# Loading x in four transposing transfers per stage, with a new stored order of the operations, in a fused long-convolution and memory-attention kernel

## The chip, the cores and the metric

The kernel runs on one core of a Trainium2 chip. The core has five engines with instruction streams of their own: TensorE (PE), VectorE (DVE), ScalarE (ACT), GpSimd (POOL) and SyncE (SP). DMAs are issued by SP, ACT and POOL here. The metric is the device time of one execution in microseconds. Before the change its median over 11 runs is 326.55 us (325.63 to 328.15).

## The reference

Two independent computations on sequences of 2048 tokens and 640 channels, laid side by side in the output:

```python
# A: a gated long convolution
k_shift = sum over t of k_pad[:, t:t+S, :] * shift_k[:, ks-1-t]      # ks = 4
kv = k_shift * v
y  = irfft(rfft(kv padded) * rfft(ssm_k padded))[:S] + kv * ssm_D
a  = q * y
# B: attention with a compressive memory, 32 heads of 20, N = 4 stages of L = 512 tokens
for s in range(4):
    a_dot = softmax(qs ks^T * scale + causal mask) vs
    a_mem = phi(qs) M / (phi(qs) z + 1e-6)
    o     = g * a_mem + (1 - g) * a_dot
    M, z  = M + phi(ks)^T vs, z + sum phi(ks)
b = o @ wo
return concatenate([a, b], axis=-1)
```

`shift_k` multiplies taps of the previous tokens, `phi` is x+1 for positive x and exp(x) otherwise, and `g` is a sigmoid of `beta`.

## The kernel before

**Part A** goes over five blocks of 128 channels (`dp`). Each block has its own loads (`load_sk`, `load_kv`, `load_q`), a shift by matmuls on `kr` (`kshift`), forward DFTs of kv ("X") and of the filter ("K") as matmuls with `Wf` (`fwd`), butterflies and a pointwise product on DVE (`bfly`, `pointwise`, `ybfly`), and inverse DFTs with `Wi` (`inverse`) whose results are multiplied by q and stored by POOL.

**Part B** goes over eight units `u`: stage `s = u // 2` of 512 tokens, and half of the heads `u % 2`. `b_proj_chunks` (line 532) makes the operations up to the attention: `load` (line 539, once per stage, in the first half) brings x of the stage into the tile `xT`, transposed, channels on the partitions; `proj(tci)` (line 556) projects 128 tokens to K, Q and V, three groups of five matmuls with `wqkv`, which ACT copies out, and sends K and Q through a DMA transpose into `KQT` (line 567) from one of two buffers `KQ`; `bound` (line 575) makes a bound of the scores by one group of matmuls, copies it as `bT`, and POOL writes it as rows into `KQT` in four small DMAs (lines 592 on); `mem` (line 596) updates the memory. `b_attn_chunks` makes the scores in the PSUM region `st`, their exponentials `ET` on ACT, the product with V, and, after the second half of a stage, four DMA transposes of the result `o_s` into `oT` (`outt`, line 681) and the output projection (`outproj`).

`xT` is one tile with one buffer, [128, 5, 512]. In stage 0 x is loaded as it stands and transposed by PE. In stages 1 to 3 a single DMA transpose on SP's queue fills the whole tile (line 542); it may start when the last projection of the stage before has read the tile, and every projection of its stage waits for it:

```python
if s > 0:
    nc.sync.dma_start_transpose(out=xT[:], in_=self.x[L * s:L * s + L, :])
```

**The order.** No engine instruction is issued where these functions are written. A recorder collects every operation with what it must come after, found from the bytes that it reads and writes; matmuls on one PSUM bank that follow each other are one operation. Then `Recorder.emit` (line 197) issues them in the sequence of `ORDER` (line 703), a stored list of operation numbers that was found offline by a search. So each engine's stream, and SP's and POOL's queues, stand in that sequence, and since every call is made in line 216, all rows of the profile show L216; tiles tell them apart. An engine works its stream in order: an instruction that waits holds up what is behind it. PSUM has one region `st` of four banks and four single banks `w`; `take` and `per_bank` hand them out as the sequence goes.

Of the kernel before, what the change touches and what calls it, by code (L numbers as in the profile page):

```python
# [21 lines left out]
S = 2048; D = 640; C = 512; P = 1024  # L22
# [253 lines left out]
class K3:  # L276
# [255 lines left out]
    def b_proj_chunks(self, u):  # L532
        nc = self.nc
        V = nc.vector
        s, half = u // 2, u % 2
# [3 lines left out]
        def load():  # L539
            xT = self.ring("xT", [128, 5, L])  # L540
            if s > 0:
                nc.sync.dma_start_transpose(out=xT[:], in_=self.x[L * s:L * s + L, :])
            else:
                xn = self.ring("o_s", [128, 4, H, DH])[:].rearrange("p t h d -> p t (h d)")
                nc.scalar.dma_start(out=xn, in_=self.x[0:L, :].rearrange("(t p) c -> p t c", p=128))
                for cc in range(5):
                    px = self.bank("w")
                    for tci in range(4):
                        nc.tensor.matmul(px[:, 128 * tci:128 * tci + 128], lhsT=xn[:, tci, 128 * cc:128 * cc + 128], rhs=self.ident[:], start=True, stop=True)
                    if cc % 2:  # L550
                        nc.scalar.copy(out=xT[:, cc, :], in_=px)
                    else:
                        V.tensor_copy(out=xT[:, cc, :], in_=px)
            self.xT = self.xTs[s] = xT
# [41 lines left out]
        def mem():  # L596
# [10 lines left out]
            V.tensor_tensor(out=dst[:, :, :, 0:DH + 1], in0=src[:, :, :, 0:DH + 1], in1=mt[:, :, :, 0:DH + 1], op=ALU.add)  # L607

        ch = [(load, 0.1)] if half == 0 else []
        ch += [(proj(t), 3.0) for t in range(4)] + [(bound, 4.0)]  # L610
        if s < NS - 1:
# [89 lines left out]
BANKS = {"st": (1, 2048), "w": (4, 512)}  # L701
SUMMED = ("X",)
ORDER = (
    'c-jTQ17H{c3<SVWKAG)x=-k=1jn1~&*|u%lwr$(CZQmtUA`W6BEW#lIA|n!j;!vbUM1)2dI1GYN2#?g7Qj=*Cjf)tFid33H(`Zr+(&U;`b7^+Xp?NhWN^4q8uZa+dbeci4Xmpg-teQ>p'
    'YbxZ^0-8~aY9=kG(NIQ<p_t~@!dg(vYiVTGQplqfw1^hcl3GGbX+^E1Ns$bdH5QViuGZ6FO@rc^6&aBe>5&P!kO66t4cU<yxseVzkOg@VfJr)8M`#I@#7M2CiID^;P+zNPRn3ch$d3j('
    'L91&K6h#e<hbcN$M`?VNLm8CC3>~dwbb(IO@fwVYI#U<wSe>r3v;b!7GF_#sb&jsk<ysiyv;xXwp4QenT1%s#rmobvx>#Fl8=bFzwK}SzA{uICEYTWRs_Qf+)@mgb#ColQYS^i}v=AC;'
    'V{M{MQ6F{DR2!hV*2WY}!bD8Q8eOE#&`d+L9@=YTG(ijPq0LbTJ+&cPpqn;AO?20=tc3~qr{HdFsjYN_Zqkj~R@>=VjKdi0#&`&)VJfC$Cc<;G&OjGcM&K6hs^Qo{J8EkLp(XZcE6hS0'
    '%*A|k(#|>$p&5!{xB&gMzxL9Fh|bw?4$$7Z2yGFSa}b4nG#cBXuSRA}Zp1*1!9g0x1dPQ14%SUb$VB{sxJ=4#NPwUCjvcxa+jP5b)%|)vS7RksVKLTV3HItfU5>R_hZR_ggL+6)u_+Jh'
    'MLnWJv>Df9s9w@#IH?;D!Y=59&e(<23}Q-l#Zf(`X&8_32}#RgI$XQql%`{PCT4qH)rce;GYPM0BqpPA8#W_3w_*#rqbE|Z2YRCyn((sj!AE?>7lfcAGBPtWF#|v0H~!!k{^B1xpgjWR'
    'GY;c4VzVu;XdIr_>v{xdbT7`J9rxje=3*A^$3f)g0UXyu$jWRKq4dE`?T75Vr6xyl94B!?RZid(jv)_2%UN~F%X1n=ZfiG&l2$y6b7;-;+8-CR4ZARr+|lq7St7_?jUqi5Q3mmzCPYit'  # L710
    'kxuN+`x;3eXipBtL(RcQ+KZie0XuLWL-1Jp;)!<UCG_J(<m3<*<zNnFZ{}k$4&XrcWqvki3*JNl7Gz--VNB`30qD=+9Ej~0!I4ZN_2sGd;UElSalX`8Qi89vBVXt}mSja%;z*3)D2~E3'
    'R$wWP=5&tbIF4s&2J^MXmNyzlYOp5nvkWJ2A|LP}AMvf$mZ_Y?$sCF)EXQGZ$=58;=lV?RNnLr$8Jx)*7>?(>jyHV8XRO7_{K_h<&2Nk<b@-VtScp|wjb-_fA6S=P_@1zNj3)J1pYtj9'
    'iMMbYzjz0~`G*a77Y*4|mhvx`F|7Qf+e*IWDu$Ege8&}h%;*wBYRNTR#bwlx!BSJMU<49NL-|Rw2GU5HNMli(#qSKZCk$srZ8mAetfI}~T&`wuD`7vlhI@GraV3m}w@?-!VJ)=9lSYg$'
    '5iFvu<vQNS1MFiY%OvG3v+QRDOCxQhl^kGX+s(AHhfmO2T1Z=IDKV@%V_GbWZDnmeA0nY7m1L4mGDv#KC<_=Q3z<^N*g<aKAui%#K1De@%p-h;jZ7|^m`YMeYH23XEUHDZ=vG}uW2o$x'
    '%{(d1C5vR0A(CCP$s^>HC9Gz@^s9c*ANpH=>O0-SZ~9(8>Q=Us_Ogx1t+XAGLvm26SXB#=4wAxpN=e(!VRBe<NH0ksN4bO5Z6|lJl*O?c7T3B<Evsqut+vIt1lGu2qlq=P239~C+GFIG'
    'mexa>+A-F%W75Ko%5k3L5qX0U3$S=r$C_DhX>N5bsr8YB_F0ozpuNBs&1mhclAYjwJ1!?AktMcP_7ZKZt8|u*lF2^lTRg{ieIc(9WR<O(bdh&RX`SR0(_33>ZyoGCQdtJ;XsPWqJ6UGC'
    '$OD$eE-{zolY-LP(pXw6B>kkX9JJha+z#1Z87{e`vvsvR(#>+qKIvk4WsmHZla|L0+X*{nBP6e7wQQEevRe)-ET`<M<+HPv-_FTs86$nIpPjQaa$btcSt%m@Wq{<g>vrC**$wM&7i_HD'
    'wgNW5#z}9xXnpL86|^HZQI6UOn<OLco(;5gR$K~MVJjv@th5ZW!FE9|$`Csx!)&;Xl*w|Qr{#{_wfpwK9@<bVB^Nl#M#*R!W8-CtOtc9y$;Mi2kLhuIvc>W#HdV&icq<{(<dL1WGxpe~'
    '+D%L7(`}mFvN;y$bFI9@_ZgPJ2T4hJDbr=9%#sQ+LuT46n`dWOMlRWWi|4N;i7&8QGF#?ISvkvvcG(u$ZFy?X?V0`2C-wp5<Q!kvVtZ*-B)LzpMY6<}+AFIlDg3o1^|YSM-`EXF=WlJX'
    '43t!!+HcBdOXFWGqc5{cvQU=DQmHD-WVYRryK<9X?H0e;J9}@J<ez2n5BAY+^9ol;CeP}beYs@wRg&E=%LBP0@T+_%^m}rR=HKnUT$Ss*CO_?m-Qjf+SN~->Jf}zU`SMEUNo83eH+YxT'  # L720
    'WUl1(TplcWJhw;o6}HNj+e-T&U*xGgk>B>mR?1^pEsx}@{E(j#&b!+;Suf!|f`6AD_R0R*23aR-#XXdV_AtIidRkcTWzXcfe3Vb}OCtJb$>+Z%zrT?v9@XE;TPf@BWs{Wi0$$Lgd366H'
    'J0!>p`Bo|HDZQkZ@{Mwt(7*Cec8cm|5smBVJ&|Yd08i|ty@(g}GG5g~YZ%=oVYQft)AC-yi+c$VuQ5E>D|!Ttq!BfWR`YsZ-#1ug-)L2QldZMQR^3-yO|Rh%e2uNMhF;6J+AayDrc~E0'
    'wnetfdTZphy^crLN*+V&dSl;aO?<oUu$|V_ciA4>YrCzPH}@7EU88DCkE5+TrY6+Z9!sNXT#c>!EI`|Oh_~^M-rn1JXYb^J+QGYcSC6OhwTE}}-rn7NdIC+PeZ7zO@_ydm{{zzes$>'
)


# [73 lines left out]
```

## Time and profile before

| | |
|---|---|
| median of 11 runs | 326.55 us (325.63 to 328.15) |
| the profiled execution | 327.24 us, of it span 325.1 us |
| mean granted TensorE clock | 0.963 |
| DMA | 42.58 MB in 89891 packets, 131 GB/s over the span |
| SP's queue (q1) | 78512 packets, 25.91 MB |
| POOL's queue (q0) | 5488 packets, 12.44 MB |

The span runs from the first to the last instruction of the profiled execution. The page gives each engine's busy time in it, the chain of work that ended last followed back from the end, groups of instructions by tile, and DMA issues with their time to landing. `w<-wqkv,xT` is a projection matmul into a bank `w`; `st<-KQT` is a score matmul; `xT<-in_B_x_dram` is the load of x. A row of a wait names who waited, for whom, the total, the number and the longest. A DMA in SP's timeline shows the time that its issue took on the queue's engine, not the transfer; the chain and the DMA rows show the time until it landed.

### The profile page before, as it was taken

What the parts mean: (1) busy time and instruction counts of PE and PEld (TensorE: products, weight loads), DVE (VectorE), ACT (ScalarE), POOL (GpSimd) and SP (SyncE); (2) the same over time, 40 slices, a digit from 0 to 9 for tenths busy, and PEclk for the clock granted to TensorE, in tenths of its full rate; (3) what the DMA queues carried; (4) which work ended last, traced back from release to release, by engine and by line L of the source; (5) the groups of instructions that cost most, each with busy time, mean ns of one, the idle gap of its engine ahead of it and who ended that gap; (6) DMA issues with size and microseconds to landing.
All of it is one profiled execution on the core that took longest, in us unless ns stands there. A gap on an engine that the chain in (4) does not pass through costs nothing.

```text
span 325.1 us, 11830 instructions
## 1 busy us (share of the span) xinstructions
PE 283.4 (87%) x5182; PEld 202.2 (62%) x5182; DVE 248.3 (76%) x382; ACT 259.1 (80%) x347; POOL 82.5 (25%) x138
## 2 busy tenths in 40 slices
PE   2849979999998997997999996499899999887984
PEld 2536557677676775664787774167667676664662
DVE  1135761898997877999989879139999999899951
ACT  2255489989998996999979996179997999886822
POOL 8000200610550001306430045400041036103333
PEclk9997999999999998999999999599999999996999
DMA  8799967577973979357536999834019456102255
GB/s 213 178 229 192 238 154 140 141 153 191 211 191 117 148 128 159 87 87 159 146 70 122 131 172 186 171 62 73 2 34 135 105 127 115 40 18 67 78 111 155
DMA packets 89891, 42.58 MB, mean 131 GB/s; under 512 B 78928, under 2 KB 85776, under 8 KB 89712
## 3 DMA queue, kind: packets, MB, share of 16 engines
q1 hardware_dynamic: 78512, 25.91, 44.7%
q0 software_dynamic: 5488, 12.44, 15.0%
q10 hardware_dynamic: 5840, 3.49, 4.6%
q8 instruction: 40, 0.66, 0.9%
q14 instruction: 11, 0.09, 0.1%
HBM read 14.16 MB, written 5.24 MB: 60 GB/s over the span
## 4 chain that ended last, share of the span: by engine, by line
PE 34%; issue 18%; DMA 17%; ACT 16%; DVE 9%; ACTq 2%; POOL 2%; SPq 1%; DVEq 0%; POOLq 0%
PE w L216 30%; ACT ET L216 7%; PE st L216 5%; DMA KQT<-KQ 4%; DMA xT<-in_B_x_dram 4%; DMA kr<-kr 3%; DMA KQT<-bT 2%; DVE S L216 2%; DMA out_dram<-outa 2%; ACTq L216 2%; ACT KQ L216 2%; ACT PqT L216 2%; ACT F L216 2%; POOL out_dram L216 1%; DVE Kh L216 1%
## 5 line engine op out<-in xcount | busy, mean ns | idle before, releaser
L216 ACT ACTIVATE ET<-st 128x2048 bf16<-128x2048 f32 (+1 forms) x96 | 155.2, 1617 | 11.1 <-PE st L216 10.1
L216 PE MATMUL w<-wqkv,xT 128*128 128x320 bf16 x480 | 79.6, 312 | 9.5 <-DMA xT<-in_B_x_dram 7.5
L216 PEld LDWEIGHTS <-xT 128*128 128x128 bf16 x480 | 45.5, 101 | 33.6 <-DMA xT<-in_B_x_dram 7.8
L216 ACT CAST F<-w 128x512 bf16<-128x512 f32 x80 | 46.0, 620 | 8.1 <-PE w L216 7.6
L216 PEld LDWEIGHTS <-ET 128*128 128x128 bf16 x1280 | 40.0, 96 | 8.5 <-issue 6.6
L216 PEld LDWEIGHTS <-Wf 128*128 128x128 bf16 x400 | 36.8, 99 | 11.4 <-issue 4.5
L216 PE MATMUL w<-Va,ET 128*128 128x21 bf16 x1280 | 42.8, 173 | 1.2 <-ACT Va L216 0.4
L216 ACT CAST KQ<-w 128x320 bf16<-128x320 f32 x64 | 26.4, 439 | 19.7 <-PE w L216 15.9
L216 DVE TENSOR_TENSOR S<-S 128x2048 bf16<-128x2048 bf16 (+1 forms) x40 | 37.4, 944 | 0.2
L216 PE MATMUL w<-vt,Wf 128*128 128x256 bf16 x240 | 35.6, 275 | 0.6 <-ACT KQ L216 0.5
L216 PEld LDWEIGHTS <-later 32*128 32x128 bf16 x1536 | 19.3, 92 | 25.8 <-issue 23.8
L216 PE MATMUL st<-KQT 21*128 21x512 bf16 (+3 forms) x512 | 34.8, 300 | 0.0
L216 POOL DMA_DIRECT2D KQT<-bT x32 | 16.5, 519 | 70.4 <-ACT bT L216 38.9
L216 PE MATMUL st<-later 32*128 32x32 bf16 (+1 forms) x1536 | 26.9, 180 | 7.4 <-ACT ET L216 6.7
L216 POOL DMA_DIRECT2D out_dram<-outa x20 | 15.9, 798 | 61.9 <-DVE outa L216 44.5
L216 PE MATMUL w<-wo,oT 128*128 128x320 bf16 x160 | 26.5, 312 | 2.9 <-DVE outa L216 1.7
L216 DVE RECIPROCAL rr<-w 128x32 f32<-128x32 f32 (+1 forms) x32 | 10.5, 327 | 19.9 <-PE w L216 19.4
L216 POOL DMA_DIRECT2D vt<-in_A_v_dram x16 | 12.4, 777 | 48.3 <-PE w L216 47.0
L216 PE MATMUL w<-kT,Wf 128*128 128x256 bf16 x160 | 23.7, 281 | 0.7 <-DVE o L216 0.5
L216 DVE TENSOR_TENSOR S<-Xh,Kh 128x4096 bf16<-128x4096 bf16 x10 | 22.7, 2283 | 0.1
L216 ACT CAST outb<-w 128x320 bf16<-128x320 f32 x32 | 13.3, 440 | 10.9 <-PE w L216 10.8
L216 PEld LDWEIGHTS <-oT 128*128 128x128 bf16 x160 | 15.3, 100 | 10.1 <-issue 4.2
(75 smaller groups left out, 430.7 us busy)
## 6 DMA issues: line engine op xcount, KB each, us to landing
qd<-in_A_q_dram POOLq DMA_DIRECT2D x20, 128.0 KB, 4.1
out_dram<-outa POOLq DMA_DIRECT2D x20, 128.0 KB, 3.1
out_dram<-outb POOLq DMA_DIRECT2D x16, 160.0 KB, 2.8
vt<-in_A_v_dram POOLq DMA_DIRECT2D x16, 128.0 KB, 3.7
kT<-in_A_ssm_k_dram POOLq DMA_DIRECT2D x4, 512.0 KB, 6.4
kr<-kr SPq DMA_DIRECT2D x10, 198.0 KB, 4.1
kr<-kr SPq DMA_DIRECT2D x5, 264.0 KB, 5.0
Wf<-c_wf ACTq DMA_DIRECT2D x4, 256.0 KB, 6.9
```

The costliest lines, as they stand in the source:

```text
L216: f(*fargs, **fkw)
```

## The change

The load of x in stages 1 to 3 becomes four DMA transposes of 128 tokens each, still on SP's queue, each into its own quarter of the tile. The recorder sees nine more operations, and each quarter depends only on the projections of its own 128 tokens. The stored sequence is replaced by another one, found by a search in which the assumed landing times of transfers were lengthened per kind of transfer. Nothing else differs.

```diff
         def load():
             xT = self.ring("xT", [128, 5, L])
             if s > 0:
-                nc.sync.dma_start_transpose(out=xT[:], in_=self.x[L * s:L * s + L, :])
+                for t in range(4):
+                    nc.sync.dma_start_transpose(out=xT[:, :, 128 * t:128 * t + 128], in_=self.x[L * s + 128 * t:L * s + 128 * t + 128, :])
...
 ORDER = (
-    'c-jTQ17H{c3<SVWKAG)x=-k=1jn1~&*|u%lwr$(CZQmtUA`W6BEW#lIA|n!j;!vbUM1)2dI1GYN2#?g7Qj=*Cjf)tFid33H(`Zr+(&U;`b7^+Xp?NhWN^4q8uZa+dbeci4Xmpg-teQ>p'
...
+    'c-jTQ17HvU5Czb?fB$kVyOwP%+qP{ko6ELs+qP}nw%vP)VG>(nNhAp;k)^mqkN^=0BN4?#C6rLYOBx9+VI>WcAqi3;IpRoaM3HC`T~Z(^(jp~tA{T;?1L=?+g^@_IA{&xQcH~2T<VI;^'
...
 )
```

Decoded, the new sequence has the same operations as the old one, with the nine new transfers, at moved places. On every engine neighbours are exchanged over short distances, and many stretches are unchanged. Places that the prediction speaks of, in the new build:

- Start: on ACT's stream the activation table load stands before the first copy of `xT` and the load of V's weights behind it, and three of the four `Wf` loads follow the copies; before, two of them and all of `wqkv`'s first half stood ahead of the table load. On SP the K weights of the second half (`loadw1`) stand third instead of ninth. On PE the first projections are P0.2 Q, P0.2 K, P0.1 K, P0.3 Q, P0.2 V, P0.4 K, P0.1 Q (unit.token block and what is projected) where they were P0.2 Q, P0.2 K, P0.4 K, P0.1 K, P0.1 Q; a projection of unit 1 comes before the memory update of unit 0.
- Stage 2: SP's queue has quarter 1 of x, an `oT` transpose, a `kr` transpose, quarter 0, quarter 2, an `oT` transpose, a `kr` copy, quarter 3.
- Stage 3: quarter 0, two `KQT` transposes, a `kr` copy, quarter 2, an `oT` transpose, a `kr` copy, three `oT` transposes, quarter 1, quarter 3. Before, the load stood behind all four `oT` transposes and three of the five `kr` copies.
- POOL, at the same place: the first of the four rows from `bT`, two stores of `outa`, the other three rows, then loads. Before, loads of q and v stood between the rows.
- DVE: several additions of the pointwise product and of `ybfly` of block 2 stand ahead of the first score matmuls of unit 5.

More of the change, by code (lines that the diff above doesn't have):

```diff
@@ L703 @@
 ORDER = (
-    'c-jTQ17H{c3<SVWKAG)x=-k=1jn1~&*|u%lwr$(CZQmtUA`W6BEW#lIA|n!j;!vbUM1)2dI1GYN2#?g7Qj=*Cjf)tFid33H(`Zr+(&U;`b7^+Xp?NhWN^4q8uZa+dbeci4Xmpg-teQ>p'
-    'YbxZ^0-8~aY9=kG(NIQ<p_t~@!dg(vYiVTGQplqfw1^hcl3GGbX+^E1Ns$bdH5QViuGZ6FO@rc^6&aBe>5&P!kO66t4cU<yxseVzkOg@VfJr)8M`#I@#7M2CiID^;P+zNPRn3ch$d3j('
-    'L91&K6h#e<hbcN$M`?VNLm8CC3>~dwbb(IO@fwVYI#U<wSe>r3v;b!7GF_#sb&jsk<ysiyv;xXwp4QenT1%s#rmobvx>#Fl8=bFzwK}SzA{uICEYTWRs_Qf+)@mgb#ColQYS^i}v=AC;'
-    'V{M{MQ6F{DR2!hV*2WY}!bD8Q8eOE#&`d+L9@=YTG(ijPq0LbTJ+&cPpqn;AO?20=tc3~qr{HdFsjYN_Zqkj~R@>=VjKdi0#&`&)VJfC$Cc<;G&OjGcM&K6hs^Qo{J8EkLp(XZcE6hS0'
@@ L708 @@
[L708 to L723, printed above, removed]
+    'c-jTQ17HvU5Czb?fB$kVyOwP%+qP{ko6ELs+qP}nw%vP)VG>(nNhAp;k)^mqkN^=0BN4?#C6rLYOBx9+VI>WcAqi3;IpRoaM3HC`T~Z(^(jp~tA{T;?1L=?+g^@_IA{&xQcH~2T<VI;^'
@@ new lines @@
+    'Kt_~BUZj#TD2J$$2XUo@WI<^uh(aiWikO7*$b{5V03}cXB~c2M5GaWynN&s<6h$#)Mm?mJ43bgmqd2M}i8MfUR6`1hDGiZaa!M}ACg~)-1W68=jO>zI^2i8`L?+21C8d<alfqI&reG>+'
+    'pe9BkzLb%&Qch-IG_uNgWR?k-h*_A4RTzV1SdA4ZCd;uBV^LJ5VF4Cm9Ohsi=3+YLW4AzNqoU-Me3D-ZNI|KMx~PL%Sd0o%UfQ57D#;R5mKst;s!2_$D%E8vV#qoak|t=1W>Qa@OMPjC'
+    '#%Lmqq=hs?V`(bQu@)`RK-#0FbU+<xiN9Ebe-K-QDKbeW%4Df44W&CGSS{&+h*n!B$XFRK<D|Xplrb_*rpr`On<+CS811kDZDl=Lp*7mbMr=YWX)P&bGj;;D3%jug?WBurL05ExSy=0c'
+    'NJi_4UT_PrPUw#i#I)Y%gD^G#vm~5#mCgun(X9*SOEl|?7}gI9WUkDXIg-fcNmLt%L5OV&C6*<y!H8o?EU_iE9oUBL*ot6TB=IeU{g7|6OZLc5`7Zl$0E=a%td%9QPWECSTG~cgEeFxc'
@@ new lines @@
+    'R>>MUgynJ=>1>5;k|8*Pix`UavQ#c%nViH1=`7u(yQH^-md4Ur4+*pkHVmn3I5OH%9K#mrC7WfN^prl*Tl&f=bh1nq%9`6%WVV#n*&<sDyM`zh+LBpvyNs{$M}EsM`6qv+gLIOP@<l#M'
+    '77Ns@mff=1UimDaB(WZrxOQ5uAf6qO)97H=u}{w6xZFTT+bXH;CPZ%`L{7*V$!qy+zZ{i=a!5|fF*%MPQ_W$a6>54wPT-WBMSgQFVCQffIW3ok(ROxLsG&62&dGVSxBhYg&GZiXSa=Q4'
+    '2znQhHKGo+dq^k=q^)(cdfLnGBa#l5-u3`}?ICj8BlNTLl1RJT5a}m9?1DVT6YP+lc2O=#9vf~YtiKJj)>hC)SV<dfL#&Xsu>n@t23iptWTUN^6}K+d)kawi9UvjrK<nyLl(N?-Z83F>'
+    '4V3LN(`MO7tD`UQ$eyFVKD5X73=Q>(HPWi~2Gwl5m9dwoY-Mevyh1D;YZGjujk8Hs&dS>$sbaCUj@7lv_SBx+Gn-;BtfEb~X*R>A+G`snv+btLu^aN%D%nSSZ^Pu1eXx2~-F{mQt8Z^?'
@@ new lines @@
+    'xLlW__RebBA8TMgEs8d@TK3I;*>|g8x8#Q{w6E64Lb0($)kPMX$`wYgw6N+7r)%t`eYUl>%3j$QTW!(wul=*=Domo`*i;*96Ro9JrG}1>nmSnD;<D7%(K1x#+B_@E>MTdFi8Zxmc3X^h'
+    '<gUcgdlFY8GoD6b6b3LVYcLGw+d5lsr5Tnfb%7nQGHkB#b%SlRXpF!Xno18^Ypu%68l71*JU3ZwYoiY&BCD~jrqvkSXX$jm#bvO@V@qwN={2cl&}6#U4%uN_Vn=MV9kuwpFArs@Ewkm8'
+    'fXD2(oz%*FD#>+=rO+#KO=9wy#AY1s*I3+Y8MP8KX=+WQAMgWT@eA8*yM03ye#B4I;cpDlteQ=O^pRxOy3C<DwS#ul9oA0U>rQ)z_ejfh+-1GAJQL_{+he`;pdQwWJf?@VHizi}J*r3a'
+    'C=)V}4cSBMvk@yW36rt`Te3A1v8T3T8zyEwCe+7LK=;}cIbp9QzrK;??4y0PDckWg8nYRbu?fE*HCwPf(=a*PGMFzUh+SBdC-gW^+HpN)XY8~c;|Zo<O1_k??8MIO#%|h0J82Gn!gmbS'
@@ new lines @@
+    '=kh|+vlib;XU)K~)?Ksly>w?rp0n)isy&#AJ(-hN>?CvXsuf^9?ZC_|s9Bhbg|wfBXn#G$f;`Q=x?A&VF5Rbjv=3j&Tj|T*?8V%=M=$Ua3-Jsu^E@xIFmp2xN9#Eqqj{N+=QS$_Xkjg)'
+    'MYXsN()=u@MR<)xIb28RJr3p&Ugu3d;0@m5L*D05KH*p$sl_;q<8+h`<RIQ<ah~NwJ;!mJq~rOVXY`boU`Z{>QaYR?cv?$qN1oM@9L4cEh8OgbP1TD!mX~dsPT*vn#EG1u(>XzBa558l'
+    'LQm{78R)Z^(qFI?U-BuZ@D-o2gihsj9nF_IOK0dzea$z#!mFIkN1V$!e9T2m<%^lz=P`ws*ZG{S6?6fYu#Dd3d0WcYn#`B+mfqn7Th0}n#(`Q^=jbARr62g7Z~2bp^n?7tMZ2vZxssn)'
+    'RabE}7jm&y)6e|E44%;|X*y5uUzy#r`ZuQaAkX4|n9ct(moL;MT3PStUA>}L^&h`e{EpqVAI$4Zb(yZvHT=n6T(0>%zvuQ<n#T+H1HGX)HH=@kdwNO3`hAVy_w0s6^vinR)UT;I{Gndg'
@@ L724 @@
+    'a30=o+AS;S^g<rXA6Rvrs}*&g&esK6)Qfo$FYK{>EjMr-*Yk@$(UrPdpQ?K(|EfRqr$+OB{HE*mgGTol{$1DTW9`onuGL2x$pid1L;C=3(8wOeqxy4wrt9>he$rnW(?4r*|E(oFj=$5m'
+    '{zj|$d#&zob)#Oh+g3&6d3;acJ9MZ1(UM-ux9TP>?U_7>m+?xT*>iej7yQ$|s@SYRSZvcU2#qA3+S7Paui|CBoLBYwUc+m8EidmCJRB-|Z4ZwKh=ho!;|;upxAcvy>zi25cW@gUdSl<t'
+    'M!uP?d?#D`7B=zS+@%J`79~PqyKdz!?qM5m>rK6xM@DlGK(HTRJ8$nDyrb{sAs*&F9%NKRL3BhzC-3a>5CgH%#bY8q;$S~xp@(<#gy`-)y{q^3z8;9UIKp1u&--`+Btm~5=pjDD2lyZ#'
+    '=0kn35BCxN9|FR!J^'
 )
```

## The prediction

> **What bounds the kernel now.** The page comes first. No engine is saturated over the whole span.
>
> ```profile
> PE 283.4 (87%) x5182; PEld 202.2 (62%) x5182; DVE 248.3 (76%) x382; ACT 259.1 (80%) x347; POOL 82.5 (25%) x138
> ```
>
> The matmul records overlap, so I priced TensorE (PE) by start-to-start spacing in the trace instead: 0.69 us for five projection matmuls, 0.88 for eight DFT matmuls, 0.45 for a score block, 0.79 for the large value block, and so on over all 427 PE operations. That is 267 us of work. PE's first matmul starts at 5.2 and its last ends at 320.3, so about 48 us are lost, mostly in pieces under 1 us where PE waits for ScalarE (ACT) or VectorE (DVE). The waits of PE show the one large piece.
>
> ```profile
> PE w L216 <- DMA xT<-in_B_x_dram: 7.5, 1, 7.5
> PE st L216 <- ACT ET L216: 6.7, 18, 0.7
> ```
>
> Columns: total us, times, longest. Eighteen waits for ACT's exponentials are short; the wait for x is one of 7.5 us. The chain that ended last, read between 186 and 222 us, says which transfer it is.
>
> ```profile
> 195.02 0.29 PE w L216 x2
> 195.31 12.65 DMA xT<-in_B_x_dram
> 207.96 0.04 issue
> 208.00 1.51 PE w L216 x5
> ```
>
> This is the third transposed load, that of the last stage (s=3). It takes 12.65 us from issue to landing; the other two landed in 5.6 and 6.3. SyncE's own timeline shows why:
>
> ```profile
> 191.62 3.60 SPq L216 DMA_TRANSPOSE oT<-o_s  x1
> 195.31 6.98 SPq L216 DMA_TRANSPOSE xT<-in_B_x_dram  x1
> ```
>
> An issue that costs 1.2 to 1.3 us elsewhere costs 3.60 here, and that of x 6.98: the queue is backed up by the copies of kr, four oT transposes, and GpSimd's loads. Everybody pays, as the busy times by stretch show (length, PE, PEld, DVE, ACT, POOL, granted clock, DMA share, GB/s):
>
> ```profile
> 200.00:203.50 3.50, 0.55 (x5) 0.18 (x2) 3.43 (x6) 1.16 (x2) 3.40 (x6) 0.82 1.36 207
> 203.50:208.00 4.50, 0.00 (x0) 0.00 (x0) 0.97 (x3) 0.00 (x0) 2.54 (x5) 0.50 1.10 220
> 208.00:212.00 4.00, 4.00 (x33) 1.89 (x34) 0.00 (x0) 2.14 (x2) 0.68 (x1) 0.50 0.30 75
> ```
>
> PE, ACT and DVE all stop, and PE comes back at a granted clock of 0.50. From 216 on DVE is the fullest engine (19.76, 19.58, 18.78 and 19.72 us of each 20 from 220 to 300), so what is lost here isn't caught up. Before that, ACT is (18.4 to 19.9 of 20 in most stretches).
>
> **The split itself.** One 640 KB transpose per stage becomes four of 160 KB, so nine more DMAs in three stages. The trace has this very shape from another source.
>
> ```profile
> oT<-o_s SPq DMA_TRANSPOSE x16, 3.6
> xT<-in_B_x_dram SPq DMA_TRANSPOSE x3, 6.3
> ```
>
> An oT transpose is 128 x 5 x 128, as a chunk of x will be; it lands in 2.6 to 9.4 us, median 3.6. Its issue is 1.25 us, so four are 5.0 against 2.7 to 3.0 for an undisturbed load of x: 2 us more of SyncE per stage, 6 in all. They run one behind the other without adding up: the last four oT are issued in 310.62 to 315.79, and the matmuls that read them run from 313.84 on without a wait for a DMA.
>
> The Trainium skill speaks against this part: "DMA: Bandwidth & Descriptors", Rules for kernel authors, says to coalesce many small transfers into one large one, and its Anatomy section fits about 2.0 us fixed plus bytes at 436 GB/s on the GpSimd path. By that, if nothing overlapped, nine more transfers would be an estimated 18 us. The oT rows say that they overlap; no row of this trace shows chunks read from HBM.
>
> What the split buys is that a chunk waits only for the projection that reads the same 128 tokens. I took, on PE, the work listed between the last reader of the old chunk and the first reader of the new one (sum of spacings). For stage 3 before: 8.4 us for the whole load, which needed 12.65. After: 20.8, 10.1, 20.9 and 15.5 for chunks 0 to 3. Chunk 1 is the tight one: SyncE's listing has an oT, a kr copy and three more oT between the chunk issued before it and itself, 6.8 us of issues of which 4.3 pass before it may start, so 2.5 of the 10.1 are gone; 7.6 are left against 3.6 (median) to 9.4 (worst oT, in just this crowded stretch). Left over: 0 to 1.8 for the landing, more if the backed-up issues recur. I take 1.0.
>
> Stage 2: before 7.7 for the whole load, which landed in 6.3 and wasn't waited for. After, chunk 0 is tight: 9.5 less three issues (3.75) is 5.8, against 3.6 to 9.4: 0 to 3.6, taken as 0, as DMA is lighter there (109 to 123 GB/s against 207 to 220). Stage 1 has 13.9 or more for every chunk: 0.
>
> **What goes:** the stall, 7.45; and the slow clock behind it. After 208.00 three blocks of five projection matmuls and one score block start 1.45, 1.30, 1.21 and 0.66 us before what follows, where the warm spacing is 0.69, 0.69, 0.69 and 0.43: 2.1 us. Both on the path, as all engines stand.
>
> **What is late next.** The score matmuls of the following unit need rows that GpSimd writes into KQT from bT:
>
> ```profile
> 200.10 1.05 POOL L216 DMA_DIRECT2D KQT<-bT  x2 [2.10 <-ACT bT L216]
> 203.93 0.53 POOL L216 DMA_DIRECT2D KQT<-bT  x1
> ```
>
> The last is issued at 203.93 and such rows land in 6.2 us in this stretch, so about 210.1: 11.6 after the matmul they derive from ended (198.5). PE has 9.7 us of work listed in between, in both builds. So without the stall PE would be about 1.9 early. After, two stores and no loads stand between the four rows, 0.8 us shorter. I charge 1.0 (0 to 1.9).
>
> **The reordering elsewhere.** Prices and PE's total are unchanged, and outside the places named here the listing is that of before with neighbours exchanged, so I cost it by bounds. Start:
>
> ```profile
> 15.80 6.66 DMA KQT<-KQ
> 24.97 1.32 PE w L216 x16
> ```
>
> The projection of the third token block can't be copied out until this transpose frees its buffer; PE then waits until 24.97. After, two more blocks precede the Q projection that this transpose needs (1.3 us each at the slow clock there, 0.7 at the full), and a 400 KB weight load (4.0 to 4.9 us to land elsewhere on this queue) is put ahead of it. Against that, one of the two Wf loads issued just there (15.30 and 16.66) moves ahead, the activation table load moves before the copies of xT (up to 0.6 gained), and one projection block fills the hole (0.7 gained). Between -1.3 and +5; I take +1.5, nearer to the small terms.
>
> DVE: before, it stops with work at hand. Time, us, instruction, idle before it:
>
> ```profile
> 204.16 0.32 DVE L216 TENSOR_TENSOR o_s<-o 128x320 bf16<-128x320 bf16 x1
> 216.25 0.36 DVE L216 RECIPROCAL rr<-w 128x32 f32<-128x32 f32 x1 [11.78 <-PE w L216]
> 217.39 1.21 DVE L216 TENSOR_TENSOR S<-S,pr 128x2048 bf16<-128x2048 bf16 x1
> ```
>
> S<-S,pr had its inputs by 202.9 but stands behind rr. After, the stage from the bound matmul of unit 5 to its first scores lists 18.4 us of DVE work instead of 10.3, and what follows lists 94.2 instead of 102.1; ACT's 96.4 there is the next limit. This stretch takes 106.6 us now. Worth 0 to 5.7 (102.1 less 96.4); I take 2.0, nearer to none, because PE's small waits stay.
>
> **Sum**, against the profiled execution's 327.24 us (span 325.1, 2.14 around it): -7.45 - 2.1 + 1.0 (chunk 1) + 1.0 (bT rows) + 1.5 (start) - 2.0 (DVE) = -8.05, so 319.2. The median of the runs before is 326.55, 0.7 under the profiled one; I keep the larger base and say 319. All terms at their good end: 327.24 - 7.45 - 2.1 - 1.3 - 5.7 = 310.7. All at their bad end: 327.24 - 9.55 + 1.8 + 3.6 + 1.9 + 5 = 330.0.
>
> **Rivals.**
> 1. *The queue, not the size, is the delay.* For: the x packets stood behind oT's, and chunks 1 and 3 are again last on SyncE, at about the same time as the load before. If chunk 1's issue is backed up like the 3.60 and 6.98 above, it lands some 5 us late, the clock drops again, and only 3 to 4 us are gained: about 323.5. Against: chunks 0 and 2 and most kr copies go earlier. 0.14.
> 2. *Given back elsewhere.* The stall goes, but the start takes its 5 us, stage 2 its 3.6 and the DVE gains nothing: 327.24 - 9.55 + 1.0 + 1.0 + 5 + 3.6 = 328.3, or within 0.3% if one of them is smaller. For: the start's transpose is on the chain. Against: 0.7 of PE work fills the hole. 0.09 that it ends within 0.3%.
> 3. *Slower: a stall per chunk.* Each chunk is a DMA of its own with its own place in a queue that also holds oT, KQT and kr. If each read of x from HBM lands in some 12.65 us, as the load of stage 3 did, chunk 0 of stage 2 misses by 12.65 - 5.8 = 6.9 and chunk 1 of stage 3 by 12.65 - 7.6 = 5.1, each with 2.1 of slow clock: 327.24 - 9.55 + 6.9 + 5.1 + 4.2 + 1 = 334.9. It decides from a landing above about 11.5 us in both stages. Against: x landed in 5.6 and 6.3 elsewhere, whole. 0.15.
>
> Forecast 0.62, the rivals 0.14, 0.09, 0.15. Faster by over 0.3% (1 us, about what a measurement of this kernel can tell from no change) is the forecast and the first rival: 0.76; within 0.3% 0.09; slower 0.15. The range runs from 313, between the sum and its good end, to 327, leaving out the slower case and a few per cent below.
>
> **What would show it.** Right: no single PE wait for xT above 2 us; the clock at 1.00 from 195 to 215; DVE's largest idle time there under 4 us; a wait of st for the bT rows of at most 2. Wrong: a wait for xT at stage 2; PE's block now at 24.97 starting after 28; chunk issues of 3 us or more on SyncE; or waits of PE for ACT well above 6.7 in total, which would mean that the exchanged neighbours cost more than I can see here.

## The result, and the profile after

| | before | after |
|---|---|---|
| median of the executions beside each other | 326.83 us (47: 323.43 to 335.12) | 324.30 us (12: 318.20 to 329.54) |
| the profiled execution | 327.24 us, span 325.1 | 326.76 us, span 325.0 |
| mean granted TensorE clock in it | 0.963 | 0.970 |

The ratio after/before is 0.981, 95% interval [0.977, 0.986]; ratios with intervals here compare only executions within 1.5% of the fastest of their kernel, which leaves out 8 of the changed kernel's 12, while medians and ranges are over all. By medians it is 324.30 / 326.83 = 0.992. So the change gains 0.8 to 1.9%, less than the 2.3% that were forecast (319 against 326.55), and its time scatters over 11 us; a further set of six executions gained nothing by medians (after_again, below). The profiled execution lies in the upper part of that range: it shows what goes wrong in such a one, not what a 318 us execution looks like.

The waits of the changed kernel (total us, times, longest):

```profile
PE st L216 <- ACT ET L216: 8.4, 21, 0.8
PE w L216 <- DMA xT<-in_B_x_dram: 7.1, 1, 7.1
DVE o_s L216 <- DMA oT<-o_s: 3.9, 1, 3.9
```

The wait for x is still there, 7.1 us in one piece where it was 7.5. The chain that ended last and SP's timeline say which transfer it is now:

```profile
189.68 5.77 DMA out_dram<-outa
195.45 14.56 DMA xT<-in_B_x_dram
210.06 2.85 PE w L216 x10
```

```profile
189.86 5.49 SPq L216 DMA_TRANSPOSE oT<-o_s  x3
195.45 5.53 SPq L216 DMA_TRANSPOSE xT<-in_B_x_dram  x2
```

Quarters 0 and 2 were issued at 178.08 and 186.63 and are there: the first projection of stage 3 starts at 200.91 instead of 208.00. But the second needs quarter 1, issued at 195.45, and this quarter of the load takes 14.56 us, longer than the whole load before (12.65). The second starts at 210.06; before, it started at 210.11. The stall has moved by one token block. The stretches by busy time (length, PE, PEld, DVE, ACT, POOL, granted clock, DMA share, GB/s) are those shown of before:

```profile
200.00:203.50 3.50, 2.78 (x39) 1.50 (x35) 2.17 (x4) 3.08 (x4) 2.45 (x4) 1.00 1.20 122
203.50:208.00 4.50, 0.00 (x0) 0.00 (x0) 1.86 (x3) 0.99 (x2) 0.53 (x1) 0.83 1.16 144
208.00:212.00 4.00, 1.94 (x8) 1.14 (x9) 1.50 (x3) 0.00 (x0) 2.57 (x4) 0.50 1.34 192
```

PE does nothing from 203.5 to 208, and from there the clock is at 0.50 again. Look at the last two columns. The DMA share adds up the times of all packets that start in a stretch, over the 16 engines, so it can exceed 1. In the first two stretches it is about as high as before (1.20 and 1.16, before 1.36 and 1.10), yet 122 and 144 GB/s move where 207 and 220 did. GpSimd's timeline shows what else was put on them:

```profile
190.46 0.65 POOL L216 DMA_DIRECT2D kT<-in_A_ssm_k_dram  x1
193.46 1.50 POOL L216 DMA_DIRECT2D vt<-in_A_v_dram  x2 [2.36 <-PE w L216]
197.44 1.49 POOL L216 DMA_DIRECT2D qd<-in_A_q_dram  x2 [2.48 <-DVE outa L216]
198.91 0.75 POOL L216 DMA_DIRECT2D vt<-in_A_v_dram  x1
199.65 0.75 POOL L216 DMA_DIRECT2D qd<-in_A_q_dram  x1
200.39 0.53 POOL L216 DMA_DIRECT2D KQT<-bT  x1
...
205.90 0.53 POOL L216 DMA_DIRECT2D KQT<-bT  x1 [2.58 <-DMA vt<-in_A_v_dram]
208.43 1.02 POOL L216 DMA_DIRECT2D KQT<-bT  x2 [2.00 <-DMA qd<-in_A_q_dram]
```

After kT (512 KB), six loads of 128 KB are issued between 193.5 and 200.4, in the very time of quarter 1; the old order had two there, at 194.89 and 197.25, and the others between and behind the rows from bT. By the profile GpSimd itself then waits for its own loads (2.58 and 2.00 us), so the last row goes out at 208.95 instead of 203.93.

### The profile page after: what moved, and what is told of

It reads as the page before. It is cut to its first block, busy times and chain, and to the rows that moved or that the text cites. A ratio compares the mean times of both kernels' runs of the same rounds, so it can differ in the third digit from the quotient of the medians.

```text
span 325.0 us, 11839 instructions
## 1 busy us (share of the span) xinstructions
PE 281.9 (87%) x5182; PEld 200.1 (62%) x5182; DVE 248.1 (76%) x382; ACT 259.2 (80%) x347; POOL 81.4 (25%) x138
## 4 chain that ended last, share of the span: by engine, by line
PE 36%; ACT 17%; issue 16%; DMA 13%; DVE 11%; POOL 3%; SPq 3%; POOLq 0%; ACTq 0%; DVEq 0%
PE w L216 30%; ACT ET L216 9%; PE st L216 6%; DMA xT<-in_B_x_dram 4%; DVE S L216 4%; DMA KQT<-KQ 3%; ACT F L216 3%; SPq L216 3%; POOL out_dram L216 2%; ACT KQ L216 2%; DMA out_dram<-outa 2%; DMA wqkv<-in_B_wq_dram 1%; DMA kr<-kr 1%; DMA ident<-c_ident 1%; ACT PqT L216 1%
## 5 line engine op out<-in xcount | busy, mean ns | idle before, releaser
L216 PEld LDWEIGHTS <-xT 128*128 128x128 bf16 x480 | 44.5, 100 | 40.6 <-issue 11.4
L216 POOL DMA_DIRECT2D out_dram<-outb x16 | 9.3, 584 | 58.8 <-ACT outb L216 46.5
L216 DVE TENSOR_REDUCE kam<-KQT 128x4 f32<-128x2048 bf16 x8 | 18.2, 2278 | 4.7 <-DMA KQT<-KQ 4.7
```

Source lines behind the costliest of these rows:

```text
L216: f(*fargs, **fkw)
```

## Experiments

**Theories.** A, crowding: GpSimd's loads for later blocks share the DMA engines with SP's transposes, and the new order put more of them beside quarter 1. B, the queue: quarter 1 stands behind three oT transposes on SP. C: a transposing read from HBM is slow by itself. D: chance between executions.

All kernels compute everything. What is edited is the sequence, in front of `rec.emit(order)` (in whole_new_order the load of x too), by a helper that takes picked operations out and puts them behind a marked one:

```python
def behind(mark, picked):
    rest = [i for i in order if i not in set(picked)]
    at = rest.index(mark) + 1
    return rest[:at] + picked + rest[at:]
```

`vt`, `qd`, `rows`, `x`, `oT`, `kr` are the operations that load v of block 4 and q of block 2, the four rows of unit 5, the quarters of stage 3, and what SP moves beside them, in the order in which they are recorded; `kT` is the load of k of block 4, `last_row` the row of unit 5 that is issued last. In the new order `rows[0]` is the row issued last. The names are shortened here.

Each kernel left one profile. To compare them by place, I took from PE's timeline the start of the first score matmuls of units 0, 1, 4, 5 and 6 and of the last output projection. For unit 4 it is the second block of score matmuls, 2.9 us behind the first in every kernel. Intervals in us; "wait" is the total of PE's waits for x in stage 3; the times are of six executions (after: twelve).

| kernel | unit 0 to 1 | 1 to 4 | 4 to 5 | 5 to 6 | 6 to end | wait | profiled us | median (range) |
|---|---|---|---|---|---|---|---|---|
| before | 31.59 | 106.30 | 39.14 | 29.87 | 70.46 | 7.5 | 327.24 | 326.83 |
| after | 31.01 | 105.01 | 39.87 | 29.95 | 71.12 | 7.1 | 326.76 | 324.30 (318.2 to 329.5) |
| after_again | 33.18 | 104.83 | 36.02 | 29.96 | 71.34 | 5.0 | 324.88 | 327.07 (319.9 to 331.6) |
| whole_new_order | 32.44 | 105.07 | 42.07 | 29.95 | 71.76 | 9.1 | 331.72 | 328.56 (321.7 to 331.7) |
| split_old_order | 31.61 | 104.86 | 31.98 | 29.87 | 70.50 | 2.3 | 319.50 | 320.35 (319.5 to 323.4) |
| split_old_again | 31.56 | 105.66 | 33.80 | 29.87 | 70.58 | 2.8 | 320.87 | 322.80 (318.6 to 327.6) |
| loads_early_old | 30.90 | 102.97 | 35.48 | 29.87 | 70.73 | 3.4 | 319.79 | 322.32 (318.6 to 327.3) |
| loads_late_old | 29.52 | 105.62 | 30.16 | 35.75 | 71.47 | 0.5 | 321.92 | 321.40 (319.4 to 323.1) |
| loads_late_new | 33.04 | 106.44 | 29.46 | 34.95 | 71.41 | 0 | 325.14 | 324.49 (320.2 to 330.1) |
| loads_spread_new | 30.30 | 105.74 | 31.84 | 30.45 | 70.99 | 2.2 | 318.42 | 323.01 (318.1 to 326.1) |
| quarters_first_new | 35.07 | 105.46 | 33.51 | 30.89 | 70.82 | 0 | 324.82 | 323.36 (319.8 to 328.5) |
| quarters_first_old | 32.47 | 105.32 | 31.20 | 31.57 | 70.85 | 1.1 | 320.85 | 320.55 (317.5 to 321.8) |
| loads_spread_both | 32.18 | 104.58 | 29.60 | 30.62 | 71.09 | 0 | 317.38 | 320.71 (317.4 to 323.4) |
| spread_and_first | 30.07 | 107.04 | 32.05 | 30.51 | 71.50 | 0 | 321.66 | 320.58 (317.2 to 322.6) |

**after_again**, the changed kernel unedited. 

> The changed kernel itself, once more, to see which of its executions the profile shows. Its profiled execution (326.76 us) had PE waiting 7.1 us for quarter 1 of x in stage 3, while its runs spread from 318 to 330. Theory A (crowding: GpSimd's loads of k, v and q for later blocks, issued at 190 to 200, share the DMA engines with the transposes, and quarter 1 lands late): the wait is there in every execution, 4 to 8 us, median about 324. Theory B (SP's own queue: quarter 1 stands behind three oT transposes and is issued only at 195.45): the same, 5 to 8 us. Theory D (chance: the landing differs from execution to execution): another profile may show a wait under 2 us, with a time near 318.

Median 327.07 us, beside 327.08 of the kernel before on the same chip: by medians no gain, though the ratio is 0.984 [0.974, 0.993]. The wait is there again, 5.0 us; quarter 1 took 10.00 us:

```profile
197.74 10.00 DMA xT<-in_B_x_dram
```

The profiled execution fell into the middle, so D is neither shown nor excluded. New is the column "unit 0 to 1": 33.18 against 31.01 in the other profile of the same program, so the scatter has a second place.

**split_old_order**, the split alone: the code of after and the stored sequence of before, with the four transfers where the one stood. 

> The four transfers in the place of the one, everything else in the order of before: the split alone. All four quarters of stage 3 are issued one behind the other from about 195.3, behind four oT transposes. Theory B (place in SP's queue): quarter 0, first of the four, lands about a quarter into the 12.65 us of before, the wait of 7.5 us falls to 2 to 5 and the time to 321 to 324. Theory A (crowding): the quarters move no faster than the whole did while GpSimd's loads run, the wait only moves to later quarters, 5 to 8 us in sum, and the time stays at 325 to 328.

```diff
+    order = [i for n in order for i in new[n]]
```

`ORDER` is that of before, and `new[n]` holds the operations that stand for its number n: four for a load of x, one for all else.

Median 320.35 us, ratio 0.983 [0.977, 0.989], and no execution above 323.5. All four quarters are issued last on SP, behind the same four oT, as the whole load was:

```profile
191.27 2.97 SPq L216 DMA_TRANSPOSE oT<-o_s  x1
194.28 6.25 SPq L216 DMA_TRANSPOSE xT<-in_B_x_dram  x4
```

```profile
PE w L216 <- DMA xT<-in_B_x_dram: 2.3, 2, 1.6
```

```profile
xT<-in_B_x_dram SPq DMA_TRANSPOSE x4, 6.7
```

The wait falls from 7.5 to 2.3, and the stretch from unit 4 to 5 from 39.14 to 31.98. This is the wait that B gave (the time is just under its 321 to 324) and not A's 5 to 8, though the place in the queue is no better than in after: quarter 1 is issued at 196.46, in after at 195.45. So B alone can't be why after waits.

**whole_new_order**, the order alone: one load per stage in the new sequence, at the place of one of its quarters. 

> One load of x per stage, as before, with all else in the order of after (the load at the place of quarter 3, 1 and 1 in stages 1, 2 and 3): the order alone. The load of stage 3 is issued at about 195.5 on SP. Theory A and B alike: it lands at 208 to 211, PE stands 7 to 10 us for it and the time is 326 to 329, so that the order by itself gains nothing. If the order's other moves (start, DVE's additions) are what made the time shorter, it is 322 to 325 in spite of the wait.

```diff
-                for t in range(4):
-                    nc.sync.dma_start_transpose(out=xT[:, :, 128 * t:128 * t + 128], in_=self.x[L * s + 128 * t:L * s + 128 * t + 128, :])
+                nc.sync.dma_start_transpose(out=xT[:], in_=self.x[L * s:L * s + L, :])
```

Of the four places of a load in the new sequence it keeps the third, first and third in stages 1, 2 and 3.

Median 328.56 us, ratio 0.990 [0.980, 0.999], and a wait of 9.1 us, as A and B alike had it; in the profile the load takes 15.94 us:

```profile
195.55 15.94 DMA xT<-in_B_x_dram
```

By medians on one chip the split is worth 327.08 - 320.35 = 6.7 us in the old order and 328.56 - 327.07 = 1.5 in the new one, where the times scatter by 10 us and more. On another chip it was worth 326.03 - 322.80 = 3.2 us in the old order (split_old_again, below). The new order does not help; it costs most of what the split brings.

**loads_late_new**: after, with nine loads of GpSimd later. 

> After, with nine GpSimd loads (kT of block 4, four vt of block 4, four qd of block 2, 1.5 MB in all) moved behind the last of the four bT rows of unit 5, so that they are issued after about 205 and not from 190 on. SP, PE, ACT and DVE are listed as in after. Theory A (crowding): quarter 1 lands within 4 to 8 us of its issue, PE waits less than 2 us for x in stage 3, and the time is 316 to 320. Theory B (SP's queue): quarter 1 is issued at 195.5 as before and PE still waits 5 us or more, 323 to 326. Theory C (a transposing read from HBM is slow by itself): as B, with a landing above 11 us. If the loads then come too late for block 4 or block 2, a wait of DVE for vt or qd shows it.

```diff
+    order = behind(last_row, kT + vt + qd)
```

This is the sharpest test, as SP, PE, ACT and DVE are listed as in after. The DMA rows of 194 to 206 us, after first (queue: packets, MB, share of 16 engines; then issues, KB each, us to landing):

```profile
q1 hardware_dynamic: 2490, 0.61, 75.7%
q0 software_dynamic: 230, 0.73, 41.2%
...
xT<-in_B_x_dram SPq DMA_TRANSPOSE x2, 13.0
...
oT<-o_s SPq DMA_TRANSPOSE x1, 12.3
```

The same stretch of loads_late_new:

```profile
q1 hardware_dynamic: 3422, 0.97, 59.1%
q0 software_dynamic: 239, 0.40, 13.6%
...
oT<-o_s SPq DMA_TRANSPOSE x3, 4.4
xT<-in_B_x_dram SPq DMA_TRANSPOSE x2, 3.9
```

Quarters 1 and 3, from the same place of the same queue, land in 3.9 us in place of 13.0. SP's queue (q1) moves 0.97 MB in less engine time than 0.61 MB took. So neither B nor C explains this wait by itself, and A holds. PE works through the old stall at full clock (length, PE, PEld, DVE, ACT, POOL, clock, DMA share, GB/s):

```profile
203.50:208.00 4.50, 4.50 (x108) 3.25 (x98) 4.03 (x7) 4.42 (x6) 4.50 (x9) 1.00 0.45 82
```

But the median is 324.49 us, not 316 to 320, ratio 0.987 [0.979, 0.995]. In the profiles, unit 4 to 5 is 10.4 us shorter than in after, and half of that is given back behind: unit 5 to 6 takes 34.95 in place of 29.95, as the nine loads now run beside the transposes of KQ, and come late for DVE. Another 3.5 us are lost ahead of the moved loads, from unit 0 to 4, which the edit does not explain.

```profile
207.53 10.88 DMA KQT<-KQ
```

```profile
DVE vt L216 <- DMA vt<-in_A_v_dram: 4.5, 1, 4.5
```

The same KQ transposes land in 4 us or so elsewhere (4.2 at the median in after_again between 184 and 214). Here too a transpose beside those loads is slow; moving all of them moved the stall.

**loads_early_old**, the reverse: the split in the old order, with the loads placed as the new order has them. 

> The four transfers in the old order (320.35 us, PE waiting 2.3 us for x in stage 3), with GpSimd's loads of vt and qd placed as the new order has them: six of 128 KB behind each other from about 195, where the old order has two there and the rest between and behind the bT rows. Nothing else moves. Theory A (those loads crowd out the transposes): the wait of PE for x in stage 3 grows to 5 us or more and the time to 324 to 328. Theory B (the place in SP's queue decides): the wait stays at 2 to 3 and the time at 319.5 to 322.

```diff
+    order = behind(vt[2], [vt[0], qd[3], qd[0], vt[3], qd[2]])
```

Median 322.32 us (318.6 to 327.3, three of six above 324), ratio 0.978 [0.970, 0.986]. The quarters land in 9.8 us at the median instead of 6.7 to 7.2:

```profile
xT<-in_B_x_dram SPq DMA_TRANSPOSE x4, 9.8
```

Their issues take 8.54 us for four instead of 6.25, the clock is at 0.50 from 200 to 203, and unit 4 to 5 takes 35.48 instead of 31.98 and 33.80. The landings and the scatter go A's way. But the wait grew only from 2.3 to 3.4, not to 5, with the quarters issued some 4 us earlier (190.43 against 194.28), and the median lies under A's 324 to 328, just above B's 319.5 to 322: half a hit. The loads alone do not make after's stall of 5 to 7 us.

**loads_spread_new**: after, with one vt and one qd ahead of the rows, and four loads moved behind. 

> After, with four of those six loads (two vt, two qd) moved behind the last of the four bT rows of unit 5, so that one vt and one qd are left ahead of the rows, as in the old order. Theory A: quarter 1 of stage 3 lands within 8 us of its issue, PE waits less than 2.5 us for it, and the time is 318 to 322. Theory B: PE waits 5 us or more, 324 to 328. That the loads come too late for block 4, as they did when all nine were moved (DVE 4.5 us for vt), would show as the same wait again.

```diff
+    order = behind(rows[0], [vt[0], qd[3], vt[3], qd[2]])
```

Quarter 1 lands in 7.75 us and the wait is 2.2, as A gave them; unit 4 to 5 takes 31.84 and unit 5 to 6 stays at 30.45: nothing is given back. The profiled execution has 318.42 us. The median over six, 323.01, does not follow (A gave 318 to 322), ratio 0.981 [0.972, 0.989], so something else scatters in the new order.

**quarters_first_new**: quarters 1 and 3 ahead of three oT. 

> After, with quarters 1 and 3 of x of stage 3 moved ahead of the last three oT transposes on SP's queue, so that quarter 1 is issued at about 191 and not at 195.5. GpSimd's loads stay. Theory B: quarter 1 lands by 199, no wait of PE for x above 1 us, 318 to 321. Theory A: quarter 1 still runs beside the loads of kT and vt and takes 9 us or more, but has 4.5 us more time, so that 2 to 4 us of the wait are left, 322 to 325. The oT transposes then land later; a wait of DVE for o_s above the present 3.9 us would be what that costs.

```diff
+    order = behind(kr[-2], [x[1], x[3]])
```

Median 323.36 us, ratio 0.983 [0.976, 0.990]. No wait for x is left in stage 3. Quarter 1, issued at 194.44 (not 191), lands in 6.78 us, at 201.22; four of the six loads of vt and qd are issued only from 200.47 on. This is B's row and not A's 9 us, though the time is A's. So an earlier place on SP's queue ends the wait too: after's stall needs both the late issue and the loads beside it. The profiled execution still has 324.82 us, and the table shows where: 35.07 us from unit 0 to 1. The chain there:

```profile
55.58 3.10 DMA kr<-kr
58.74 0.46 SPq L216
59.25 9.10 DMA kr<-kr
68.48 0.64 PE w L216 x7
```

and GpSimd at that time:

```profile
55.96 2.28 POOL L216 DMA_DIRECT2D vt<-in_A_v_dram  x3 [13.71 <-DVE tq L216]
58.23 0.75 POOL L216 DMA_DIRECT2D qd<-in_A_q_dram  x1
58.97 0.55 POOL L216 DMA_DIRECT2D kT<-in_A_ssm_k_dram  x1
```

A copy of kr that the shift of block 1 waits for takes 9.10 us beside kT and qd, which the old order issues later (in the profile of before kT at 63.82, behind the first of unit 1's rows, and this qd at 86.18). It looks like the same pattern at a second place.

**quarters_first_old**: the split in the old order, the quarters ahead of the last oT. 

> The four transfers in the old order, with the four quarters of stage 3 moved ahead of the last of the four oT transposes, so that they are issued from about 191.3 and not 194.3. All theories: the 2.3 us that PE still waits for quarter 0 go, and the time is 317 to 319.5. If it stays at 320 or above, PE then waits for the bT rows or the landing is set by the traffic and not by the issue.

```diff
+    order = behind(x[3], [oT[2]])
```

The wait falls from 2.3 to 1.1, but the median is 320.55 us, ratio 0.982 [0.977, 0.988]: as split_old_order, not the 317 to 319.5 expected. Issued 3 us earlier, at 191.31, the quarters land in 8.8 us and not 6.7 at the median, and quarter 0 has landed at 200.89 instead of 201.00. That is the second reading: the traffic sets the landing, more than the issue does.

**split_old_again**, split_old_order unedited. 

> The split alone in the old order once more, beside the others on one chip: 319 to 323 us with a median near 320.5, as in the first look. If it lies above 323 that first look was chance.

Median 322.80 us, within the 319 to 323, ratio 0.986 [0.981, 0.991], one execution at 327.6. Of the twelve executions of the split in the old order one is above 324; of the eighteen of after ten are. Medians of these: 320.9 and 324.8.

**loads_late_old**: the kernel before, unsplit, with the same nine loads later. 

> The kernel before, one transfer per stage and the old order, with the same nine GpSimd loads (kT of block 4, four vt of block 4, four qd of block 2) behind the four bT rows of unit 5. Theory A (crowding): the whole load of stage 3, issued at 195, lands in 5.5 to 7 us in place of 12.65, and PE waits 2 us or less for it, without any split; 3 to 5 us come back where the loads are then late, so 321 to 325. If the size of the transfer is the delay, the load still takes 10 us or more and PE waits 5 or more.

```diff
+    order = behind(last_row, kT + vt + qd)
```

Median 321.40 us, none above 323.1, ratio 0.986 [0.982, 0.990]. As A gave it, the whole load of 640 KB lands in 6.8 us instead of 12.65, and PE waits 0.5 us for it:

```profile
xT<-in_B_x_dram SPq DMA_TRANSPOSE x1, 6.8
```

```profile
PE w L216 <- DMA xT<-in_B_x_dram: 0.5, 1, 0.5
```

As in loads_late_new, 29.87 becomes 35.75 behind it. Still, moving nine loads without any split gains at least what the whole change did: 326.03 - 321.40 = 4.6 us by medians on one chip, against 326.83 - 324.30 = 2.5. By itself the size of the transfer did not make it late.

**loads_spread_both**: loads_spread_new, and kT and one qd behind the rows of unit 1. 

> After, with four loads of vt and qd behind the bT rows of unit 5 as before, and with the loads of qd (128 KB) and kT (512 KB) that the new order puts ahead of the bT rows of unit 1 (issued at 58 to 61, just when SP copies kr of block 1) behind those rows. The stretch from the first scores of unit 0 to those of unit 1 took 30.3 to 35.1 us in the six profiles of the new order and 30.9 to 32.5 in the four of the old. Theory A, now also for the spread of the new order's times: that stretch takes 30 to 31.5 us, the one from unit 4 to unit 5 31 to 33, and the time is 317 to 320 with no run above 323. If the spread has another source, runs above 324 remain.

```diff
     order = behind(rows[0], [vt[0], qd[3], vt[3], qd[2]])
+    order = behind(last_row1, [qd0, kT1])
```

`last_row1` is the last row of unit 1, `qd0` and `kT1` are a load of q of block 0 (128 KB) and that of k of block 1 (512 KB).

Median 320.71 us, 317.4 to 323.4, ratio 0.980 [0.976, 0.985]. Ten executions of eighteen lay above 324 in after, two of six in loads_spread_new, none here. The median lies just above A's 317 to 320, and one execution above its 323. Unit 4 to 5 takes 29.60, PE's longest wait in 185 to 225 is 0.6, and the old stall is gone:

```profile
203.50:208.00 4.50, 4.32 (x108) 3.04 (x108) 3.82 (x8) 3.92 (x5) 3.90 (x6) 1.00 1.32 152
```

Unit 0 to 1 took 32.18 in this profile, not the 30 to 31.5 expected, so that place isn't proved by it; what shows is that the slow end of the range has gone, here and in the next kernel: none of twelve executions lies above 324. That speaks for crowding behind D as well. Which of the moved loads does it is not shown.

**spread_and_first**, both repairs. 

> As the one before, and quarters 1 and 3 of x of stage 3 ahead of the last three oT transposes: the best version that the runs so far point to. 316 to 319 us, no wait of PE for x above 1 us in stage 3.

```diff
+    order = behind(kr[-2], [x[1], x[3]])
```

Median 320.58 us, 317.2 to 322.6, ratio 0.980 [0.975, 0.984]: no better than the one before, and not the 316 to 319 expected. No wait for x is left, but the last oT land later (6.84 us, on the chain), so 32.05 from unit 4 to 5. Both beat the two kernels by their medians, and are level with the split in the old order.

## Why the prediction was right or wrong

The sign is right and the range (313 to 327) holds the median of 324.3; the time of 319 is 5 us off, and the forecast case, in which the stall goes, is not what the profile shows. So the time fell within the range without the mechanism that was forecast for it, which is luck; after_again's median of 327.07 falls just outside.

- **The stall, -7.45.** The whole load's stall went: the first projection starts 7.1 us earlier. It came back at quarter 1.
- **Quarter 1, "I take 1.0".** This is the step that failed. It set 7.6 us that were left against landings of 3.6 to 9.4, from oT rows, and got at most 1.8. Measured: 14.56 and 10.00 us, a wait of 7.1 and 5.0. The right quarter was named and its distance was about right; the landing was taken from rows under the old traffic, while the new order changes that traffic. The working read GpSimd's listing only for the rows from bT ("two stores and no loads stand between the four rows, 0.8 us shorter"), and took as a gain that the loads had left that place, although it had named GpSimd's loads among what backed up the queue before. They had gone ahead of the rows, beside quarter 1. loads_late_new shows it: the same issue, without the loads, lands in 3.9.
- **The slow clock, -2.1.** It hung on the stall, and came back with it: a clock of 0.50 from 208 to 212.
- **The rows from bT, +1.0.** No wait of PE for them shows. They were issued up to 208.95, 5 us later than before, and not 0.8 earlier; quarter 1 hid it.
- **The start, +1.5.** First scores at 41.87 and 41.64 us against 41.43: 0.2 to 0.4. The block at 24.97 started at 24.25.
- **DVE's additions, -2.0.** Nothing shows. Unit 5 to 6 takes 29.95 against 29.87; from unit 4 to 6 the new order without a wait for x above 2.2 takes 60.2 to 64.4 in five kernels, and the old one with the split 61.9 to 63.7, within the scatter of both.
- **Stage 2, 0.** Right in the profile of after: no wait of PE for x there. Four other profiles of the new order show 0.2 to 1.2 us. (The 109 to 123 GB/s were means over 20 us, set against stretches of 3.5 and 4.5; from 120 to 128 us 166 to 167 moved.) Unit 1 to 4 is 1.3 shorter than in the profile of before, where PE had waited 1.7 behind a store of outa; that this is the change's is not shown.
- **Not priced:** the end, 0.7 to 0.9 longer, and the scatter from unit 0 to 1 (30.3 to 35.1 in the six profiles of the new order with its loads there unmoved). One trace shows crowding at kr's copies; with those loads moved it took 32.18 and 30.07, so the cause of this scatter stays open.
- **The rivals.** Rival 1 gave the time, 323.5 with quarter 1 some 5 us late and the clock down, and was put at 0.14. Its mechanism, the place on SP's queue, is half of the cause: quarters_first_new ends the wait by the place, but split_old_order issues all quarters at the end and hardly waits. Rival 3, slower with 12.65 us for every read from HBM, needs such landings in stage 2 too; there quarters took 4.0 to 4.5 at the median. Its limit of 11.5 us leaves out the slow clock and the 1.0 of its own sum; with these 5.2 us it is 8.9. Of the signs named, a wait above 2, the clock and an issue above 3 us (quarter 1's took 4.21) spoke against the forecast, as did DVE, idle for 5.4 us (limit 4); PE's waits for the exponentials rose from 6.7 to 8.4.

The order made against longer landing times did bring two quarters forward, but also GpSimd's loads, and so lengthened the landings of what it had left last. That the search meant this is not known; that the loads do it is shown by moving them both ways.

The Trainium skill, "DMA: Bandwidth & Descriptors", Rules for kernel authors, says to coalesce many small transfers into one large one; in the runs the split is worth 6.7 and 3.2 us in the old order and 1.5 in the new, and no cost of it shows. The same page, Queues, rings and completion order, says that a DMA engine takes turns between its queues, a whole packet at a time; the packets that the profile shows of GpSimd's loads are mostly of 4096 bytes and those of the transposes of 256, which would fit, but no run here varied packet sizes.

## What to carry to other kernels

In this kernel a landing time depended on the traffic beside the transfer more than on its size. When an order moves loads on one queue, list which transfers of the other queues run in the same microseconds, and price those again. A transfer that looks too large may only be crowded; moving loads that could wait showed it here, where the whole load then landed in 6.8 us and not 12.65. And spread such loads out rather than put them off together, since a late bunch crowds what follows (5 us given back).

## What was not expected of the hardware

- The 160 KB transposing reads of stage 3 that are issued last landed by what GpSimd loaded beside them, in medians of a profile: 3.9 us without the loads of kT, vt and qd, 6.4 to 8.8 with kT and two of 128 KB ahead of the rows, 9.8 to 13.0 with kT and six (14.56 for the slowest). In quarters_first_new, issued ahead of most of the six, they took 6.5.
- It is not the sum of the bytes: between 200 and 203.5 us the DMA share is 1.20 in after and only 122 GB/s move, where 207 did before. In the trace the packets of SP's queue, mostly of 256 bytes, take 78 ns on average from 196 to 200 us in after and 19 ns in loads_late_new.
- What in the DMA engines makes them slow stays open, as does what a 318 us execution of the changed kernel looks like, since neither of its profiles fell on one.
